# One correction operation in the first scan, early raw weights, and three unread products

## The chip, the cores and the metric

The kernel runs on one core of a Trainium2 chip. The metric is the device time of one execution in microseconds (us); lower is better. The engines are TensorE (PE in the profile, its weight loads PEld), VectorE (DVE), ScalarE (ACT), GpSimd (POOL) and SyncE (SP), whose queue issues the DMAs.

## The reference

Three stages follow one another, for 4 batches of 768 tokens. The first is a gated linear attention with 8 heads of 48 channels: per token a complex decay is normalised, a state is multiplied by it and takes up k v, and q reads it out.

```python
mag = np.sqrt(a_re * a_re + a_im * a_im)
scale = np.minimum(mag, 0.999) / (mag + 1e-06)
new_re = ar * S_re - ai * S_im          # per token t
new_im = ar * S_im + ai * S_re
S_re, S_im = new_re + kv, new_im
y[:, :, t] = np.einsum('bhd,bhde->bhe', q[:, :, t], S_re)
```

The second adds the real part of a two-dimensional Fourier transform to its input, normalises over the 384 channels and applies a two-layer network (384 to 1536 to 384). The third mixes over tokens (768 to 256 to 768) and then over channels again. All of it is float32.

## The kernel before, in words

The state is not stepped through token by token. For each chunk of 96 tokens the kernel forms the running complex product P of the decays, outward from the chunk's middle, in 48 steps plus one; q and k are multiplied by P or by its inverse, and the attention inside a chunk and from one chunk to the next is then matrix products. Four batches pass through the same program, and batch 0 has a scan of its own, `first_scan` (L330), which this change touches.

**The first scan.** 128 partitions hold head and chunk pairs, one half of them for each direction. `SL4` cuts the 49 steps into 12 slices of four and one of one, counted from 0. `st_a` loads the decays (`raw`) and q with k (`xx`), `st_b` to `st_e2` make the normalised multipliers A two slices ahead (ScalarE, GpSimd and VectorE together; L432 is GpSimd's last product of it, L401 the one before), and `st_f` is one step: two VectorE products (L453 into PSUM, L456 into `yt`) and their sum (L459) into P in PSUM. After a slice `st_s` squares P on ScalarE (L468) and makes |P|^2 (x) and 1/|P|^2 (r) with a logarithm and an exponential; GpSimd multiplies x by r (L473), which would be 1 if r were exact. `st_r` (L489) makes the correction (x r - 2) r, `st_x` (L495) multiplies the second half of `xx` by its negative, and `st_y` (L482) forms y, which is stored to DRAM (`kn`) and transposed on TensorE by `st_t` (L506). The function `vq` chains all VectorE operations of the scan in the order of the code, and `line_up` says which of them stand behind which step of the slice: eight places, two for each step, the first of the two ahead of the step's sum and the second behind it. L489 stands in place 6, ahead of the last sum, and L495 in place 7, behind it. In slices 8 to 11, `warm` (L316) puts two products with an identity into a PSUM tile that nobody reads.

**Around it.** After the scan `stage1` goes through 8 chunks of the attention (`ch_load`, `ch_sc`, `ch_u`, `ch_y`); the reloads of y from DRAM are L808, those of v L802. `stage2` makes the Fourier transform (`folds`, `mirrors`, `dft`, then products at L1115) and the normalisation, and `mlp`, `tok1` and `tok2` are the dense products (L999, L1021), from about 167 us to the end.

**Weights.** They come as 56 pieces of 64-bit numbers of 384 KB (`wL`, piece p, j). `convert` (L185) is a generator that a caller moves on by one stage at a time: the load (L190) into a tile of the tag T; two ScalarE operations on the halves (L198 to PSUM, L203 in place); a VectorE shift (L205); a GpSimd sum and a VectorE merge (L207, L210); then ScalarE makes a rounded first half (L216), GpSimd the rest (L217), and both are stored to `wscr` (L218), from where later batches load them. `early` is the list of the first eight pieces (p 0 to 3); their products go to tiles of the tags w1 and w2 (four buffers each, handed out in turn by `ws.place`). `tick` starts and moves conversions: two pieces at the start of the chunk loop and two after each of the first chunks (`CF`).

**The order of the work** is not that of the code. The framework plans a timeline ahead of the run: on each engine it takes, of the instructions that are ready by its plan, the one with the lowest number (`Prio`: conversions in the stream BACK come behind the first chain), and the engine then runs them strictly in that order. `after` adds an edge that holds for this planning only. Waits between engines and on buffers are put in by the framework.

Of the kernel before, what the change touches and what calls it, by code (L numbers as in the profile page):

```python
# [10 lines left out]
I32 = mybir.dt.int32  # L11
# [37 lines left out]
def with_ap(ap, offset, dims):  # L49
    return bass.AP(ap.tensor, ap.offset + offset, [list(ap.ap[0])] + [list(d) for d in dims])  # L50
# [3 lines left out]
def attn_fft_mixer_kernel(ctx: ExitStack, tc: tile.TileContext, aL, xL, vL, wL, qN, kN, vN, arN, aiN,  # L54
# [61 lines left out]
    def r32(ap):  # L116
        return ap.bitcast(F32)
# [48 lines left out]
    def marked(x):  # L166
        if stream[0] != CHAIN:
            mark[0] = x

    def after(x, y):  # L170
        tc.add_manual_dep(x.ins, y.ins.name, HOLD, reason="order of the streams")

    def hold(x):

        if mark[0] is not None:
            after(x, mark[0])
# [3 lines left out]
    def rest(x):  # L180

        if rests[0] is not None:
            after(x, rests[0])

    def convert(p, j, w=None, held=True, far=False):  # L185


        n = 384
        t = alloc("T", [128, 3 * n], I32, name="cvt")
        x = sp.dma_start(out=t[:, 0:2 * n], in_=wL32[p][:, 768 * j:768 * j + 768])  # L190
        if held:
            hold(x)
        yield
        raw = t[:, 0:2 * n].rearrange("p (n t) -> p n t", t=2)
        lo, hi, a = raw[:, :, 0], raw[:, :, 1], t[:, 2 * n:3 * n]
        if far:
            x = palloc("p" if far == 1 else "c", [128, n])
            se.activation(out=x, in_=hi.bitcast(F32), func=ACTF.Copy, scale=2.0 ** -112)  # L198
            top = hi = x.bitcast(I32)
        else:  # L200
            top = a
            se.activation(out=a.bitcast(F32), in_=hi.bitcast(F32), func=ACTF.Abs, scale=2.0 ** -112)
        se.activation(out=lo, in_=lo.bitcast(U32), func=ACTF.Copy, scale=2.0 ** -29)  # L203
        yield
        rest(ve.tensor_scalar(out=a, in0=top, scalar1=3, scalar2=None, op0=ALU.logical_shift_left))  # L205
        yield
        x = ge.tensor_tensor(out=a, in0=a, in1=lo, op=ALU.add)  # L207
        if rests[1] is not None:
            after(x, rests[1])
        rest(ve.scalar_tensor_tensor(out=a, in0=hi, scalar=-0x80000000, in1=a, op0=ALU.bitwise_and, op1=ALU.bitwise_or))  # L210
        if w is None:
            parts = t[:, 0:2 * n].bitcast(F32R).rearrange("p (k n) -> p k n", k=2)
        else:
            yield
            parts = w(p, j)
        se.copy(out=parts[:, 0, :], in_=a.bitcast(F32))  # L216
        ge.tensor_tensor(out=parts[:, 1, :], in0=a.bitcast(F32), in1=r32(parts[:, 0, :]), op=ALU.subtract)  # L217
        sp.dma_start(out=wscr[p][j], in_=r32(parts))  # L218

# [108 lines left out]
    def first_scan(t, knd, qk):  # L330
# [12 lines left out]
        def vq(x):  # L343

            if last[0] is not None:
                after(x, last[0])
            last[0] = x
            return x
# [114 lines left out]
        def st_s(i):  # L463

            d = t[i]
            n = d["n"]
            e = alloc("e", [128, n, 2, 48], name="ss")
            se.activation(out=e, in_=d["P"], func=ACTF.Square)  # L468
            x, r = e[:, :, 0, :], e[:, :, 1, :]
            ge.tensor_tensor(out=x, in0=x, in1=r, op=ALU.add)  # L470
            se.activation(out=r, in_=x, func=ACTF.Ln, bias=wee)
            se.activation(out=r, in_=r, func=ACTF.Exp, scale=-1.0)
            ge.tensor_tensor(out=x, in0=x, in1=r, op=ALU.mult)  # L473
            d["ss"] = e

        def st_y(i, k):
# [8 lines left out]

        def st_r(i):
            e = t[i]["ss"]
            o = with_ap(away[0], 192, [(48, t[i]["n"]), (1, 48)])
            vq(ve.scalar_tensor_tensor(out=o, in0=e[:, :, 0, :], scalar=-2.0, in1=e[:, :, 1, :], op0=ALU.add, op1=ALU.mult))  # L489
            t[i]["inv"] = o  # L490

        def st_x(i):
            d = t[i]
            x = d["xx"][:, :, 1, :]
            vq(ve.scalar_tensor_tensor(out=x, in0=d["inv"], scalar=-1.0, in1=x, op0=ALU.mult, op1=ALU.mult))  # L495

        def st_t(i, k):
            if not qk:
                qk.append(alloc("qk", [128, 12288], name="qkt"))
            qkt = qk[0][0:112]  # L500
            d = t[i]
            s0 = d["s0"]
            y = ybuf[k][i % 2]
            ps = palloc("s", [112, N4, 128])
            for j in range(N4):
                te.transpose(ps[:, j, :], y[:, j, 0:112], ident)  # L506

            def rows(ap, o, step, g=()):
                return with_ap(ap, o, [*g, (96, 8), (768, 8), (step, N4)])

            def cols(o, g=()):
                return with_ap(ps, o, [*g, (8, 8), (1, 8), (128, N4)])
            if k == 0:
                se.copy(out=rows(qkt, s0, 1, [(64 * 96 + 48, 2)]), in_=cols(0, [(64, 2)]))
            else:
                se.copy(out=rows(qkt, 64 * 96 + 47 - s0, -1), in_=cols(0))
                se.copy(out=rows(qkt, 48 + s0, 1), in_=cols(64))
# [30 lines left out]
        def line_up(i):  # L548

            fs = [[] for _ in range(8)]  # L550
            if 1 < i:
                fs[0] += [lambda: st_y(i - 2, 1), lambda: st_t(i - 2, 1)]
            if 0 < i < NS:
                fs[2] += [lambda: st_y(i - 1, 0), lambda: st_t(i - 1, 0)]
                fs[6] += [lambda: st_r(i - 1)]
                fs[7] += [lambda: st_x(i - 1)]
            if i + 2 < NS:
                at = (1, 4, 5)
                if not i:
                    at = (5, 6, 7)  # L560
                    fs[2] += [lambda: st_d(1)]
                    fs[3] += [lambda: part1(3), lambda: st_e1(1)]
                    fs[4] += [lambda: st_e2(1)]
                fs[at[0]] += [lambda: st_d(i + 2)]
                fs[at[1]] += [lambda: st_e1(i + 2)]
                fs[at[2]] += [lambda: st_e2(i + 2)]
            return [lambda f=f: [g() for g in f] for f in fs]
# [8 lines left out]
        part1(2)  # L576
        for i in range(NS):
            n = t[i]["n"]
            if i:
                part1(i + 3)  # L580
            fs = line_up(i)
            for j in range(n):
                st_f(i, j, fs[2 * j:2 * j + 2])
            st_s(i)
            for f in fs[2 * n:]:
                f()
            if WS <= i < 12:
                warm(W0, ybuf[0][i % 2].rearrange("p s c -> p (s c)"))
            if i == NS - 1:
                line_up(NS)[0]()  # L590
# [442 lines left out]
    def stage2(b, space):  # L1033
# [64 lines left out]
        folds(len(XP[b]) - 1, *XP[b][-1])  # L1098
        x = mirrors(*NR[1])
        if b == 0:  # L1100
            marked(x)
            rests[0], rests[1] = x, None
            for _ in range(5):
                tick(0)
            rests[0] = None
# [323 lines left out]
```

## Time and profile before

| | us |
|---|---|
| median of 3 runs (lowest, highest) | 1052.88 (1051.49, 1053.27) |
| profiled execution | 1054.68 |
| its span, first to last instruction | 1052.6 |
| TensorE products busy | 966.8 (92%) |
| VectorE busy | 744.2 (71%) |
| ScalarE busy | 511.5 (49%) |
| GpSimd busy | 392.2 (37%) |

The span is that of one profiled execution; what lies outside it (2.1 us) is start and end. Busy times of engines overlap. In the rows further down a timeline line gives start, duration, engine, line of the kernel, operation, output and inputs (buffer numbers left out), and in brackets the idle time before it with what ended it. The granted clock of TensorE is a share of 2.4 GHz: 1.00 is that level and 0.50 is 1.2 GHz.

### The profile page before, as it was taken

The page shows a single profiled execution, that of the slowest core. Times are in us where ns is not written, and L with a number is a line of the kernel's source. Part 1 is how long each engine was busy: PE and PEld are TensorE (multiplying, and loading weights), DVE is VectorE, ACT ScalarE, POOL GpSimd, SP SyncE. Part 2 cuts the span into 40 slices and gives each one's busy share as a digit, 9 for nine tenths or more (in the row PEclk, how much of TensorE's full clock was granted, in tenths as well). Part 3 has the DMA queues.
Part 4 walks back from the last instruction along what each step waited for, and adds up shares of the span by engine and source line. Part 5 has one row for each costly group of instructions (what it writes and reads, how often), then busy time and mean ns, then how long its engine had stood idle before and what let it go on. Part 6 is the DMA issues. An engine that isn't in the chain of part 4 may idle for free.

```text
span 1052.6 us, 21046 instructions
## 1 busy us (share of the span) xinstructions
PE 966.8 (92%) x7306; PEld 916.2 (87%) x7306; DVE 744.2 (71%) x2070; ACT 511.5 (49%) x1447; POOL 392.2 (37%) x541
## 2 busy tenths in 40 slices
PE   1469989998989899999999999999999999999997
PEld 0238877997889789999998999999899999999997
DVE  6986867998897697999768979984854433433332
ACT  6752557777875336788424757832252212111211
POOL 6632774565464772455237412414521002000000
PEclk9986899999989889999999999999999999999999
DMA  7226964777667743675654446665305344534422
GB/s 228 50 81 178 304 240 167 232 252 247 195 193 224 213 128 109 198 213 178 185 152 161 129 142 192 200 171 130 112 31 181 120 138 143 164 126 132 168 91 78
DMA packets 98337, 173.09 MB, mean 164 GB/s; under 512 B 10928, under 2 KB 57904, under 8 KB 97712
## 3 DMA queue, kind: packets, MB, share of 16 engines
q1 hardware_dynamic: 98224, 171.67, 52.7%
q8 instruction: 60, 0.98, 0.4%
q14 instruction: 53, 0.43, 0.1%
HBM read 132.31 MB, written 39.32 MB: 163 GB/s over the span
## 4 chain that ended last, share of the span: by engine, by line
PE 65%; DVE 15%; DMA 7%; ACT 5%; POOL 4%; issue 3%; SPq 1%; POOLq 0%; ACTq 0%; DVEq 0%
PE l L1021 23%; PE l L999 22%; DMA cvt<-wL 4%; PE s L817 2%; PE s L693 2%; PE s L1115 1%; PE l L1247 1%; DVE qkt L1064 1%; DVE h L1012 1%; DMA kn<-y 1%; PE s L1229 1%; DVE y L482 1%; DMA wscr<-w 1%; DVE cvt L210 1%; PE s L1247 1%
## 5 line engine op out<-in xcount | busy, mean ns | idle before, releaser
L1021 PE MATMUL l<-w,h 128*128 128x384 f32 x1728 | 327.9, 341 | 1.4 <-DVE h L1012 1.4
L999 PE MATMUL l<-th,w 128*128 128x384 f32 x1152 | 315.4, 342 | 2.3 <-DVE h L1012 2.0
L1021 PEld LDWEIGHTS l<-w,h 128*128 128x128 f32 x1728 | 301.0, 190 | 2.5 <-DVE h L1012 1.7
L999 PEld LDWEIGHTS l<-th,w 128*128 128x128 f32 x1152 | 210.2, 189 | 5.2 <-DVE h L1012 3.0
L999 PE MATMUL l<-tl,w 128*128 128x384 f32 x576 | 194.8, 338 | 0.0
L1003 ACT ACTIVATE h<-l 128x384 fp32r<-128x384 f32 x192 | 93.3, 487 | 207.5 <-PE l L999 206.8
L1024 DVE TENSOR_TENSOR u<-u,l 128x384 f32<-128x384 f32 x192 | 105.2, 548 | 71.7 <-PE l L1021 71.3
L1012 DVE SCALAR_TENSOR_TENSOR h<-l,h 128x384 fp32r<-128x384 f32 x160 | 88.3, 552 | 89.2 <-ACT h L1003 88.9
L999 PEld LDWEIGHTS l<-tl,w 128*128 128x128 f32 x576 | 109.0, 189 | 0.2
L207 POOL TENSOR_TENSOR cvt<-cvt 128x384 int32<-128x384 int32 x56 | 57.9, 1036 | 29.4 <-DVE cvt L205 25.7
L217 POOL TENSOR_TENSOR w<-cvt,w 128x384 fp32r<-128x384 f32 x44 | 45.8, 1042 | 49.4 <-ACT w L216 42.9
L1214 POOL TENSOR_TENSOR xl<-u,xh 128x384 fp32r<-128x384 f32 x18 | 18.1, 1014 | 96.3 <-ACT xh L1213 96.3
L203 ACT ACTIVATE cvt<-cvt 128x384 int32<-128x384 uint32 x56 | 31.2, 558 | 38.4 <-DMA cvt<-wL 38.4
L506 PE MATMUL s<-misc,y 128*112 128x128 f32 x64 | 14.5, 369 | 38.1 <-DVE y L482 32.8
L506 PEld LDWEIGHTS s<-misc,y 128*112 128x112 f32 x64 | 9.3, 176 | 44.6 <-POOL ss L470 21.0
L642 POOL TENSOR_TENSOR A<-raw,tm 128x144 f32<-128x144 f32 (+1 forms) x51 | 26.4, 517 | 53.3 <-DVE yt L667 19.1
L1010 POOL TENSOR_TENSOR h<-full,h 128x384 fp32r<-128x384 f32 x32 | 32.7, 1021 | 35.8 <-ACT full L1009 34.9
L666 DVE TENSOR_TENSOR p<-p,A 128x144 f32<-128x144 f32 x144 | 44.4, 308 | 1.3
L624 POOL TENSOR_TENSOR tm<-tm 128x144 f32<-128x144 f32 (+1 forms) x51 | 25.1, 494 | 51.3 <-ACT tm L623 48.8
L693 PE MATMUL s<-misc,y 128*112 128x128 f32 x222 | 36.5, 276 | 5.1 <-DVE y L677 3.6
L668 DVE TENSOR_TENSOR p<-p,yt 128x96 f32<-128x96 f32 x144 | 37.4, 260 | 2.3
L817 PE MATMUL s<-qkt 112*96 112x96 f32 x328 | 38.6, 266 | 0.2 <-DVE gt L785 0.2
(314 smaller groups left out, 1993.8 us busy)
## 6 DMA issues: line engine op xcount, KB each, us to landing
w<-wscr SPq DMA_DIRECT2D x180, 384.0 KB, 3.6
cvt<-wL SPq DMA_DIRECT2D x56, 384.0 KB, 4.6
wscr<-w SPq DMA_DIRECT2D x44, 384.0 KB, 3.3
Kn<-kn SPq DMA_DIRECT2D x56, 192.0 KB, 4.2
kn<-y SPq DMA_DIRECT2D x96, 96.0 KB, 2.4
raw<-aL SPq DMA_DIRECT2D x48, 144.0 KB, 3.6
xx<-xL SPq DMA_DIRECT2D x48, 144.0 KB, 3.8
V<-vL SPq DMA_DIRECT2D x32, 144.0 KB, 3.1
```

The lines of the kernel that those rows point to most:

```text
L207: x = ge.tensor_tensor(out=a, in0=a, in1=lo, op=ALU.add)
L217: ge.tensor_tensor(out=parts[:, 1, :], in0=a.bitcast(F32), in1=r32(parts[:, 0, :]), op=ALU.subtract)
L666: ve.tensor_tensor(out=cur, in0=prev, in1=A[:, j, 0:3, :], op=ALU.mult)
L668: ve.tensor_tensor(out=cur[:, 0:2, :], in0=cur[:, 0:2, :], in1=y, op=ALU.add)
L693: te.transpose(ps[:, j, :], y[:, j, 0:112], ident)
L817: te.matmul(out=ps[:, j, :], lhsT=K[:, hc, :], rhs=Q[:, hc, :])
L999: te.matmul(out=ps, lhsT=w1[:, wi, kt * 128:kt * 128 + 128], rhs=x[g][:, kt, :], start=(n == 0), stop=(n == 8))
L1003: x = se.activation(out=hi, in_=ps, func=ACTF.Relu)
L1010: ge.tensor_tensor(out=lo, in0=full, in1=r32(hi), op=ALU.subtract)
L1012: ve.scalar_tensor_tensor(out=lo, in0=ps, scalar=0.0, in1=r32(hi), op0=ALU.max, op1=ALU.subtract)
L1021: te.matmul(out=ps, lhsT=hs[m][:, hi, tt * 128:tt * 128 + 128], rhs=w2[:, wi, :], start=(n == 0), stop=(n == 8))
L1024: ve.tensor_tensor(out=u[tt], in0=u[tt], in1=ps, op=ALU.add)
```

## The change

Four edits. `st_s` gets a GpSimd product: r times the second half of `xx`, in place. `st_r` and `st_x` become one VectorE operation, (2 - x r) times that, in place 7. `preload` allocates eight tiles of w1 and w2, and in slices 5 to 8 issues two loads each of the early pieces into them; `convert` then reads the raw data there, keeps a T tile only for its intermediate, and its store to `wscr` is put on the list `kept`, which is stored after the last mirror of batch 0's `stage2`. And `st_t` puts three unread products of 512 columns behind the transposes of slice 11's first half.

```diff
+    ahead, kept = {}, []
+
+    def preload(n):
+
+        done = []
+        for p, j in early:
+            if (p, j) not in ahead and len(done) < n:
+                ahead[p, j] = alloc("w1" if j == 0 else "w2", [128, 768], I32, name="wr")
+                done.append(sp.dma_start(out=ahead[p, j], in_=wL32[p][:, 768 * j:768 * j + 768]))
+        return done
+
     def convert(p, j, w=None, held=True, far=False):
         n = 384
         t = alloc("T", [128, 3 * n], I32, name="cvt")
-        x = sp.dma_start(out=t[:, 0:2 * n], in_=wL32[p][:, 768 * j:768 * j + 768])
-        if held:
-            hold(x)
+        a = t[:, 2 * n:3 * n]
+        if (p, j) in ahead:
+            t = ahead[p, j]
+        else:
+            x = sp.dma_start(out=t[:, 0:2 * n], in_=wL32[p][:, 768 * j:768 * j + 768])
+            if held:
+                hold(x)
         yield
         raw = t[:, 0:2 * n].rearrange("p (n t) -> p n t", t=2)
-        lo, hi, a = raw[:, :, 0], raw[:, :, 1], t[:, 2 * n:3 * n]
+        lo, hi = raw[:, :, 0], raw[:, :, 1]
...
-        sp.dma_start(out=wscr[p][j], in_=r32(parts))
+        if (p, j) in ahead:
+            kept.append((wscr[p][j], r32(parts)))
+        else:
+            sp.dma_start(out=wscr[p][j], in_=r32(parts))
...
             ge.tensor_tensor(out=x, in0=x, in1=r, op=ALU.mult)
+            if d["m"]:
+                w = d["xx"][:, :, 1, :]
+                ge.tensor_tensor(out=w, in0=w, in1=r, op=ALU.mult)
             d["ss"] = e
...
         def st_r(i):
             e = t[i]["ss"]
-            o = with_ap(away[0], 192, [(48, t[i]["n"]), (1, 48)])
-            vq(ve.scalar_tensor_tensor(out=o, in0=e[:, :, 0, :], scalar=-2.0, in1=e[:, :, 1, :], op0=ALU.add, op1=ALU.mult))
-            t[i]["inv"] = o
-
-        def st_x(i):
-            d = t[i]
-            x = d["xx"][:, :, 1, :]
-            vq(ve.scalar_tensor_tensor(out=x, in0=d["inv"], scalar=-1.0, in1=x, op0=ALU.mult, op1=ALU.mult))
+            x = t[i]["xx"][:, :, 1, :]
+            vq(ve.scalar_tensor_tensor(out=x, in0=e[:, :, 0, :], scalar=2.0, in1=x, op0=ALU.subtract, op1=ALU.mult, reverse0=True))
...
             for j in range(N4):
-                te.transpose(ps[:, j, :], y[:, j, 0:112], ident)
+                tp = te.transpose(ps[:, j, :], y[:, j, 0:112], ident)
+            if 11 <= i and (i, k) != (11, 1):
+                warm(3 if i == 11 else 1, y.rearrange("p s c -> p (s c)"), tp)
...
-                fs[6] += [lambda: st_r(i - 1)]
-                fs[7] += [lambda: st_x(i - 1)]
+                fs[7] += [lambda: st_r(i - 1)]
...
         for i in range(NS):
             n = t[i]["n"]
+            if i in (5, 6, 7, 8):
+                for x in preload(2):
+                    after(x, t[i - 1]["scan"])
...
         x = mirrors(*NR[1])
         if b == 0:
+            for o, v in kept:
+                after(sp.dma_start(out=o, in_=v), x)
             marked(x)
```

## Rows read from the trace of the kernel before

**Rows 1.** Windows by stage: length, busy us (count) per engine, clock, DMA share, GB/s.

```profile
21.39:52.89 31.50, 14.74 (x51) 9.47 (x52) 29.29 (x114) 24.23 (x73) 20.42 (x30) 1.00 0.22 51
52.89:75.00 22.11, 13.88 (x51) 6.38 (x50) 20.33 (x79) 11.54 (x37) 8.01 (x15) 0.92 0.28 70
75.00:95.00 20.00, 17.18 (x148) 14.73 (x149) 9.76 (x30) 5.45 (x18) 2.95 (x5) 0.50 0.45 135
95.00:140.00 45.00, 41.18 (x573) 36.55 (x572) 37.47 (x86) 23.59 (x54) 27.14 (x27) 0.92 0.96 305
140.00:167.40 27.40, 22.68 (x127) 17.64 (x126) 20.18 (x60) 16.57 (x48) 19.60 (x24) 0.94 0.46 172
167.40:1052.60 885.20, 856.01 (x6362) 830.72 (x6360) 613.60 (x1656) 415.61 (x1182) 300.98 (x412) 0.99 0.52 162
```

**Rows 2.** Timeline of VectorE, a steady slice's ends; last two from slice 11.

```profile
35.70 0.25 DVE L456 TENSOR_TENSOR yt<-p,A 128x96 f32<-128x96 f32 x1
...
36.32 0.27 DVE L459 TENSOR_TENSOR p<-l,yt 128x96 f32<-128x96 f32 x1
36.49 0.35 DVE L495 SCALAR_TENSOR_TENSOR xx<-l,xx 128x192 f32<-128x192 f32 x1
37.14 0.27 DVE L453 TENSOR_TENSOR l<-p,A 128x96 f32<-128x96 f32 x1 [0.30 <-ACT ss L468]
...
42.39 0.27 DVE L453 TENSOR_TENSOR l<-l,A 128x96 f32<-128x96 f32 x1 [0.30 <-ACT ss L468]
...
71.08 0.25 DVE L456 TENSOR_TENSOR yt<-l,A 128x96 f32<-128x96 f32 x1
71.36 0.27 DVE L459 TENSOR_TENSOR l<-l,yt 128x96 f32<-128x96 f32 x1
```

**Rows 3.** Instructions of line L489: duration ns min/median/max, first and last start.

```profile
L489 DVE SCALAR_TENSOR_TENSOR l<-ss x12: 366/392/848, 19.7 to 75.9; 128x192 f32<-128x192 f32 x12
```

**Rows 4.** Timeline of VectorE, the last step of slice 8.

```profile
56.62 0.25 DVE L456 TENSOR_TENSOR yt<-l,A 128x96 f32<-128x96 f32 x1
...
57.70 0.27 DVE L459 TENSOR_TENSOR l<-l,yt 128x96 f32<-128x96 f32 x1
```

**Rows 5.** Timeline of GpSimd, two steady slices and slice 8.

```profile
36.02 0.94 POOL L432 TENSOR_TENSOR A<-A,both 128x384 f32<-128x384 f32 x1
...
38.80 0.59 POOL L473 TENSOR_TENSOR ss<-ss 128x192 f32<-128x192 f32 x1 [0.48 <-ACT ss L472]
40.53 0.78 POOL L401 TENSOR_TENSOR tm<-tm 128x192 f32<-128x192 f32 x1 [1.14 <-ACT tm L399]
...
56.61 0.82 POOL L432 TENSOR_TENSOR A<-A,both 128x384 f32<-128x384 f32 x1 [1.08 <-DVE A L428]
```

**Rows 6.** Timeline of VectorE, the last y of the scan.

```profile
76.74 0.56 DVE L482 TENSOR_TENSOR y<-xx,l 128x384 f32<-128x384 f32 x1
```

**Rows 7.** Chain of work that ended last, from 64 to 115 us: start, us, what.

```profile
78.22 2.94 DMA kn<-y
...
81.26 2.82 DMA Kn<-kn
```

**Rows 8.** Waits from 68 to 170 us: us in total, times, longest us.

```profile
ACT cvt L203 <- DMA cvt<-wL: 17.0, 10, 4.3
```

**Rows 9.** Timeline of VectorE, the first product (L853) of four chunks.

```profile
94.09 0.56 DVE L853 TENSOR_TENSOR yc<-l,gm 48x384 f32<-48x384 f32 x1 [2.04 <-PE l L848]
...
99.38 0.56 DVE L853 TENSOR_TENSOR yc<-l,gm 48x384 f32<-48x384 f32 x1
...
107.24 0.56 DVE L853 TENSOR_TENSOR yc<-l,gm 48x384 f32<-48x384 f32 x1
...
113.38 0.56 DVE L853 TENSOR_TENSOR yc<-l,gm 48x384 f32<-48x384 f32 x1
```

**Rows 10.** Timeline of TensorE, unread products of slices 8 and 9, two each.

```profile
50.84 3.60 PE L321 MATMUL l<-y,misc 128*128 128x512 f32 x4
...
55.61 1.88 PE L321 MATMUL l<-y,misc 128*128 128x512 f32 x4
```

## The prediction

> **What bounds the kernel now.** I read the busy table by stage first, then each stage's own timeline. From 167.4 us on, the dense products fill TensorE (856 of 885 us at clock 0.99), and the change takes nothing out of them [rows 1]. So the question is how early that stretch can begin. Ahead of it lie the first scan (to 75 us), the chunk loop and transforms (75 to 140), and the second transform (140 to 167.4). In the scan TensorE is idle half of the time while VectorE works 29.3 of 31.5 us: the scan is VectorE's. From 75 to 95 TensorE is nearly always busy, but at 0.50, the 1.2 GHz level. From 95 to 140 the DMA engines are 0.96 busy [rows 1].
>
> In the scan's timeline one slice of four tokens takes 42.39 - 37.14 = 5.25 us. Its last step has the correction L489 between yt (L456, 35.70) and the sum L459 (36.32): 0.62 us, where the bare pair takes 71.36 - 71.08 = 0.28. After the sum the next slice starts 0.82 us later, held by ScalarE's square of the same product bank; L495 (0.35 us) lies inside that wait and costs nothing [rows 2].
>
> **The change part by part.** *One correction operation.* L489 and L495 become one operation in L495's place, behind the sum; GpSimd gets one more product per slice. What goes from VectorE's path is 0.62 - 0.28 = 0.34 us a slice. What may come back: L495 reads one operand from PSUM, the new operation reads two from SBUF, as L489 did. L489 takes 0.39 us in the median but up to 0.85 [rows 3]. In the slice from 52.89 the stretch from yt to the sum is 57.70 - 56.62 = 1.08 us instead of 0.62 [rows 4], and GpSimd's L432 runs from 56.61 to 57.43 just then; the sum starts 0.27 us after L432's end [rows 5]. The new operation's place in a steady slice is 0.17 us behind the sum, and L432 runs there (36.02 to 36.96).
>
> So I count the twelve uses by their neighbours. Steady slices (2 to 7, six): the sum moves from 36.32 to 35.98, ScalarE would release the next slice at 35.98 + 0.82 = 36.80, but L432, which without L489 in its way takes 0.82 and ends at 36.84, holds the new operation. If the next slice follows L432's end by 0.27, as in rows 4, it starts at 37.11 and 0.03 us is gained; if the new operation were free, 0.34. The next step doesn't read its result, and independent steps here start before their forerunner ends (L495 0.10 us before the sum's end [rows 2]), so I take 0.15: 6 x 0.15 = 0.9 us, bounds 0.2 and 2.0. Slices 8 and 9: 1.08 - 0.28 = 0.80 goes; L432 then holds the new operation to 57.70, but the square holds the next slice to 56.62 + 0.28 + 0.82 = 57.72 anyway: 2 x 0.80 = 1.6. Slice 1 has the same collision, but GpSimd's queue is fuller there: 0.5 of 0.8. Slices 10 and 11 have no long L432: 2 x 0.3 = 0.6. In slice 12 nothing covers: a GpSimd product more (0.59 us, as L473 [rows 5]), one operation of 0.39 less: +0.2. Scan: -0.9 - 1.6 - 0.5 - 0.6 + 0.2 = -3.4 us, bounds -4.8 and -2.0.
>
> The trace shows L489 at 0.85 where it meets L432 and 0.39 elsewhere [rows 3 to 5]. The Trainium skill's "SBUF — State Buffer" (Who interferes with whom) says that a VectorE instruction with two SBUF inputs and a GpSimd instruction that reads SBUF exclude each other for the whole instruction; the trace agrees in these three slices. By the rule the merged operation pays in every steady slice for what L495 didn't; without it the six would give 2.0 and the sum would be 1.1 larger.
>
> GpSimd's twelve products cost nothing in the steady slices: it idles 1.14 us ahead of L401 [rows 5], and the new 0.59 us fits behind L473 (38.80 to 39.39). Without that cover it is 0.59 a slice, 7 us in all.
>
> *Eight raw weights early.* Eight loads of 384 KB go out in slices 5 to 8, where the DMA engines are 0.22 to 0.28 busy [rows 1]. Eight issues delay SP's stores of the scan by well under 1 us each; these have a whole slice of slack, since their buffers alternate. What they leave: first, the two loads that stood in SP's queue at the scan's end. The last y is done at 76.74 + 0.56 = 77.30 us [rows 6], its store goes out only at 78.22, and store and reload (2.94 and 2.82 us) lead straight to the chunk loop [rows 7]. I give 0.5 of the 0.9 us back, bounds 0 and 0.9. Second, the loop itself: ScalarE waits for these loads 17.0 us in ten places, 4.3 at most [rows 8], VectorE's conversion step stands behind it in order, and the loop's steps behind that. Undisturbed, a chunk takes VectorE 99.38 - 94.09 = 5.29 us; the two after it take 107.24 - 99.38 = 7.86 and 113.38 - 107.24 = 6.14 [rows 9]. With the data there both should come to 5.29: 2.57 + 0.85 = 3.4 us, bounds 0 (TensorE or the chunk's own loads hold it instead) and 4.1.
>
> The raw data lies in the buffers that the products later take, in the same order, so the conversions wait for nothing new. The eight stores of the halves move behind the last mirror (about 140 us): 3 MB, some 10 us at the 305 GB/s of rows 1, into a stretch where the DMA engines are 0.46 busy. That room covers them; without it the two loads of that time come up to 10 us later, and ScalarE's transform copies queue behind their conversions.
>
> *Three products in the last slice.* Each is half of a pair of L321: 1.88 / 2 = 0.94 us at 2.4 GHz, 1.8 at 1.2 [rows 10], so 2.8 or 5.4 us on TensorE, ahead of the last transposes, which are due about 1.5 us after the ones they follow. That is 1.3 or 3.9 us late. TensorE has about 1 us of room before the chunk loop's first product, and at the higher level its score products ahead of it are twice as fast. I take 0, bounds -2.5 (below) and +2.
>
> Sum: -3.4 - 0.5 - 3.4 = -7.3 us. The profiled execution took 1054.68 us, 2.1 of it outside its span of 1052.6; so 1047.4 in its terms, and against the median of 1052.88 about 1045.5 us.
>
> **The rivals.** (1) *The clock holds through the first chunk.* For it: the added products come where TensorE is nearly idle and the clock falls (0.92 before 75 us, 0.50 after). Against: they are followed by a wait for the reload. At 2.4 GHz the 17.2 us of work in 75 to 95 [rows 1] would halve, but VectorE's 5.29 us a chunk and the reload stay: 2.5 us more. 1043. (2) *The chunk loop doesn't shrink.* Something else, the reloads or TensorE at 1.2 GHz, holds it: only scan and start, -3.9, 1049. (3) *Given back before the dense products.* The stretch from 140 us converts other weights in the same queues, with the moved stores beside it; if they set its end, 1 us remains: 1052. (4) *Slower: ScalarE waits for raw data inside the scan.* The instructions are ordered by a planned timeline; with the data planned to be there, the first conversion step (L203) may be put between the scan's ScalarE steps, and if a load lands later than planned, the square and so VectorE stand behind it. At the 17.0 / 10 = 1.7 us of rows 8 for each of eight it is 13.6 - 7.3 = +6.3: 1059. It decides above 7.3 / 8 = 0.9 us a load. Against it: those waits were in a crowded stretch, here the engines are a quarter busy.
>
> **How the numbers follow.** Forecast 0.43, (1) 0.17, (2) 0.18, (3) 0.10, (4) 0.08, else 0.04. A measurement of this kernel tells 0.2% (2.1 us) from no change. Faster by more: forecast, (1), (2) and a little of (3), 0.80. Within: most of (3), 0.10. Slower: 0.10. Range: the forecast's own is 1043 to 1048; with (1) below and (2) and half of (3) above it is 1040 to 1052.
>
> **What would show it.** A steady slice of 5.1 us, the sum 0.28 us after yt in every slice, the new operation longer than 0.35 where it meets L432; scan slices 8 and 9 near 4.8 us; no wait of L203 on a load before 115 us; chunk periods of 5.3 us; the first dense product near 160 us. Wrong it would be if steady slices reach 5.25, if ScalarE waits for a load before 75 us, or if the dense products start early and the span doesn't follow.

## The result and the profile after

The kernel after takes 1040.74 us (median of 4 runs, 1037.56 to 1042.85), the one before 1053.08 beside it (1051.49 to 1053.56): a ratio of 0.9883, 95% interval [0.9855, 0.9911]. Forecast were 1045.5 us, with a range of 1040 to 1052. The profiled run took 1040.36 us, its span is 1038.6.

Windows of the profile after by stage, against [rows 1] (length, then busy us and count of PE, PEld, DVE, ACT and POOL, clock, DMA share, GB/s):

```profile
20.27:51.39 31.12, 14.52 (x51) 9.25 (x52) 28.91 (x110) 26.71 (x81) 23.17 (x37) 1.00 0.55 152
51.39:75.00 23.61, 17.01 (x59) 9.61 (x58) 19.74 (x77) 14.15 (x43) 11.93 (x23) 0.86 0.25 57
75.00:95.00 20.00, 18.49 (x304) 15.72 (x303) 15.64 (x42) 5.22 (x14) 5.64 (x7) 1.00 0.54 129
95.00:130.00 35.00, 31.21 (x428) 27.82 (x426) 33.62 (x74) 18.37 (x44) 24.03 (x26) 1.00 0.80 258
130.00:156.20 26.20, 21.05 (x115) 16.00 (x113) 19.11 (x57) 16.02 (x45) 18.50 (x23) 0.93 0.66 253
156.20:1038.60 882.40, 852.33 (x6362) 825.05 (x6360) 613.42 (x1655) 415.25 (x1182) 300.51 (x412) 0.99 0.53 162
```

The third row is what the sum did not have: from 75 to 95 us the granted clock is 1.00, the 2.4 GHz level, where it was 0.50, and TensorE gets through 304 products instead of 148. The early loads show in the first row's 152 GB/s. The dense stretch is the same work: 6362 products in 882 us instead of 885.

Executions of one kernel differ, and the clock differs with them: the four of the kernel after took 1037.56 to 1042.85 us at mean granted clocks of 0.993 to 0.985. Windows, landmarks and chunk periods below come from one profiled execution of each kernel. In these the start of slice 1 alone lies anywhere from 14.71 to 15.76 us, and it does not follow the edits (15.33 in the kernel before, 15.00 in `w_only` and 15.38 in `mp`, both further down), so parts of half a microsecond aren't told apart at a landmark.

The same landmarks in both traces, in us from the span's start; "expected" is the sum of the prediction up to that point:

| | before | after | moved | expected |
|---|---|---|---|---|
| last y of the scan | 76.74 | 74.69 | -2.05 | -3.4 |
| issue of its store | 78.22 | 75.27 | -2.95 | -3.9 |
| first state product of chunk 0 (L832, now L851) | 84.21 | 81.39 | -2.82 | -3.9 |
| VectorE's first product of chunk 0 (L853, now L872) | 87.88 | 82.55 | -5.33 | -3.9 |
| the same of chunk 2 | 99.38 | 90.96 | -8.42 | -3.9 |
| the same of chunk 4 | 113.38 | 101.21 | -12.17 | -7.3 |
| first dense product | 167.39 | 156.16 | -11.23 | -7.3 |
| end of the span | 1052.6 | 1038.6 | -14.0 | -7.3 |

VectorE's first product of chunks 0 to 4 in the profile after, against [rows 9] (start, us, engine, line, operation; brackets hold the idle time before):

```profile
82.55 0.56 DVE L872 TENSOR_TENSOR yc<-l,gm 48x384 f32<-48x384 f32 x1 [2.05 <-PE l L852]
...
86.75 0.56 DVE L872 TENSOR_TENSOR yc<-l,gm 48x384 f32<-48x384 f32 x1
...
90.96 0.56 DVE L872 TENSOR_TENSOR yc<-l,gm 48x384 f32<-48x384 f32 x1
...
96.08 0.56 DVE L872 TENSOR_TENSOR yc<-l,gm 48x384 f32<-48x384 f32 x1
...
101.21 0.56 DVE L872 TENSOR_TENSOR yc<-l,gm 48x384 f32<-48x384 f32 x1
```

The two periods that the loads were to shorten are 5.12 and 5.13 us, as forecast. The two ahead of them are 4.20 and 4.21 instead of 6.21 and 5.29: in these only one of VectorE's two conversion lines stands (L220 or L225), so 5.29 us was not its floor there.

The wait on the raw data, against [rows 8], from 65 to 170 us (us in total, times, longest):

```profile
ACT cvt L218 <- DMA cvt<-wL: 3.1, 3, 1.5
```

TensorE ahead of chunk 0 in the kernel before:

```profile
80.32 1.57 PE L817 MATMUL s<-qkt 112*96 112x96 f32 x8
81.69 1.49 PE L817 MATMUL c<-qkt 112*96 112x96 f32 x8
...
84.21 0.31 PE L832 MATMUL l<-V,Kn 96*64 96x48 f32 x1 [1.03 <-DMA Kn<-kn]
...
85.20 1.60 PE L817 MATMUL s<-qkt 112*96 112x96 f32 x8
```

And in the kernel after, with the unread products (L339) ahead of it:

```profile
72.95 3.30 PE L339 MATMUL l<-y,misc 128*128 128x512 f32 x6
76.09 0.60 PE L521 MATMUL s<-misc,y 128*112 128x128 f32 x4
...
78.18 0.84 PE L836 MATMUL c<-qkt 112*96 112x96 f32 x8
78.99 0.92 PE L836 MATMUL s<-qkt 112*96 112x96 f32 x8
81.39 0.23 PE L851 MATMUL l<-V,Kn 96*64 96x48 f32 x1 [1.49 <-issue]
```

The order is another. Before, the second half of chunk 0's score products stands among its state products, behind the seventh of sixteen (the group at 85.20), behind the wait for the reload. After, it stands ahead of them (78.99), where TensorE would only wait. The first VectorE product of chunk 0 follows the first state product by 3.67 us before and by 1.16 us after. No line of the diff asks for this: the planner chose it. That is the 2.5 us between the third and the fourth row of the table.

### The profile page after: what moved, and what is told of

Same layout as the page of the kernel before. It is cut to its first block, busy times and chain, and to the rows that moved or that the text cites. A ratio compares the mean times of both kernels' runs of the same rounds, so it can differ in the third digit from the quotient of the medians.

```text
span 1038.6 us, 21023 instructions
## 1 busy us (share of the span) xinstructions
PE 955.7 (92%) x7312; PEld 904.1 (87%) x7312; DVE 744.0 (72%) x2058; ACT 510.4 (49%) x1447; POOL 397.1 (38%) x553
## 4 chain that ended last, share of the span: by engine, by line
PE 62%; DVE 15%; DMA 7%; ACT 6%; POOL 5%; issue 4%; SPq 1%; POOLq 0%; ACTq 0%; DVEq 0%
PE l L1040 22%; PE l L1018 22%; DMA cvt<-wL 3%; PE s L836 1%; PE s L712 1%; PE s L1136 1%; PE l L1268 1%; DVE cvt L225 1%; DMA V<-vL 1%; DVE h L1031 1%; DMA raw<-aL 1%; DVE cvt L220 1%; DVE qkt L1083 1%; PE s L1250 1%; POOL w L232 1%
## 5 line engine op out<-in xcount | busy, mean ns | idle before, releaser
L222 POOL TENSOR_TENSOR cvt<-cvt 128x384 int32<-128x384 int32 x48 | 50.3, 1050 | 14.3 <-DVE cvt L220 11.8
L218 ACT ACTIVATE cvt<-cvt 128x384 int32<-128x384 uint32 x48 | 26.5, 557 | 27.4 <-DMA cvt<-wL 27.2
L872 POOL TENSOR_TENSOR yc<-Aa,gm 48x384 f32<-48x384 f32 x18 | 19.4, 1078 | 49.2 <-DVE Aa L862 48.9
```

## The experiments

Three kernels do one part of the change each, a fourth all but the unread products. Diffs are against the kernel after where nothing else is said.

**m_only**: the merged correction alone.

```diff
-            if 11 <= i and (i, k) != (11, 1):
-                warm(3 if i == 11 else 1, ...)
-            if i in (5, 6, 7, 8):
+            if i in ():
```

> The merged correction operation alone, no early loads, no three products. Stage theory (each edit keeps the share that the changed kernel's trace shows in its stage): the scan ends 2 to 3 us earlier, the clock in 75 to 95 us stays at 0.50, the chunk loop keeps its two long periods (7.9 and 6.1 us): -2.5 us against the kernel before. Rival (the port takes it all back): steady slices at 5.25 us and less than -1.

Measured: 1049.60 us, ratio 0.997 [0.9947, 0.9993]. Last y at 73.11, 3.6 us earlier (expected in the sum: 3.4), of which 0.6 is there already when slice 1 starts and can't be put down to the edit; slices 4 to 7 of 5.00 us, clock 0.50 from 75 to 90, first dense product at 165.7. The scan was sized about rightly; more than half of it is gone by the dense products, which start 1.7 us earlier.

**p_only**: early loads and late stores alone; the old pair of operations stands in its old places, and the GpSimd product is gone.

```diff
-            x = t[i]["xx"][:, :, 1, :]
-            vq(ve.scalar_tensor_tensor(... op0=ALU.subtract, op1=ALU.mult, reverse0=True))
+            o = with_ap(away[0], 192, ...)
+            vq(ve.scalar_tensor_tensor(out=o, ... op0=ALU.add, op1=ALU.mult))
...
-                warm(3 if i == 11 else 1, ...)
```

> The early raw weights and their late stores alone, with the old two correction operations and no three products. Stage theory: the last y's store goes out 0.9 us earlier, the two long chunk periods (7.9 and 6.1) become 5.3, the scan is 0.3 us longer by the conversion steps between ScalarE's scan steps, the clock stays at 0.50 until the loop is under way: -4 us. Rival (the loop is held by TensorE at 1.2 GHz and by its own reloads): -1.5 or less.

Measured: 1047.02 us, 0.9961 [0.9938, 0.9983]. Periods of chunks 2 and 3: 4.89 and 5.34 us instead of 7.86 and 6.14. But the last y comes at 78.80, 2.1 us later than before (0.4 of it by the start of slice 1): ScalarE's first conversion steps are planned between the scan's own, and slices 4 to 7 take 5.51 us instead of 5.25. The first dense product comes at 161.0. TensorE has the new order here, without any unread product.

**w_only**: the three products alone, merge and loads undone as in the two kernels above; the diff is against the kernel before.

```diff
+            if 11 <= i and (i, k) != (11, 1):
+                warm(3 if i == 11 else 1, y.rearrange(...), tp)
```

> The three unread products alone. Clock theory: they run at 1.2 GHz (about 5 us), the clock stands at 1.00 from about 80 us on, and the first two chunks take 8.4 instead of 11.5 us: -3 us, unless what follows waits for its loads anyway. Rival (the loads hold the loop): the clock rises as well but the waits on loads grow by as much, and the span moves by less than 1 us.

Measured: 1044.18 us, 0.9935 [0.9909, 0.996]. Clock 1.00 from 75 to 100 us, first chunk periods of 4.20 and 4.20, first dense product at 161.1. The term that I had set to nothing has the lowest ratio of the three taken alone, though its interval overlaps that of `p_only`. TensorE has the new order here too.

**mp**: the change without the three products.

```diff
-                warm(3 if i == 11 else 1, y.rearrange(...), tp)
```

> The changed kernel without the three products. Clock theory: the first two chunks are back at about 11.5 us and the clock at 0.50 up to about 90 us: 4 to 5 us slower than the changed kernel, -7.5 against the kernel before. Rival (the clock falls and rises by the spacing of the work and the faster scan alone keeps it): within 1.5 us of the changed kernel, -11.

Measured: 1044.46 us, 0.9927 [0.9897, 0.9957]; last y at 75.25, but the first product of chunk 0 at 85.86, at a clock of 0.50 up to 90 us, and the first dense product at 165.1. This one has the old order, so the 8.9 us between its first dense product and that of the kernel after are order and clock together.

**w1**: the kernel after with one product for three.

```diff
-                warm(3 if i == 11 else 1, ...)
+                warm(1 if i == 11 else 1, ...)
```

> The changed kernel with one unread product in slice 11 instead of three. Clock theory (the three keep TensorE busy long enough that the clock stands at 1.00 when the chunk loop begins): one product, 1 to 2 us, does not do it; the clock is 0.50 in 80 to 85 us, the first two chunk periods are 6 instead of 4.2 us, and the kernel is 3 to 5 us slower than the changed one, -8 us against before. Rival (any product there will do): clock 1.00, periods 4.2, the changed kernel's time.

Measured: 1043.17 us, 0.9927 [0.9901, 0.9952]. Windows from 75 to 95 us, columns as above:

```profile
75.00:80.00 5.00, 4.30 (x47) 3.60 (x46) 3.30 (x18) 1.67 (x7) 0.29 (x1) 0.86 0.56 110
80.00:85.00 5.00, 3.37 (x56) 3.18 (x58) 2.55 (x5) 0.00 (x0) 0.00 (x0) 0.82 0.48 131
85.00:90.00 5.00, 5.00 (x49) 4.22 (x46) 2.13 (x6) 0.58 (x1) 1.97 (x2) 0.50 0.62 133
90.00:95.00 5.00, 5.00 (x89) 4.55 (x88) 4.87 (x10) 2.02 (x5) 0.41 (x1) 1.00 0.26 74
```

It has the new order, and VectorE starts chunk 0 at 82.78, as after (82.55). Then the clock falls to 0.50 and chunk 0 takes 7.04 us instead of 4.20; the first dense product is at 159.0 instead of 156.2. With the order as it is, the clock that the other two products hold is worth 2.8 us between these two executions. That is a price from one pair: the profiled execution of `w1` had the lowest clock of its nine (0.979, and 1046.15 us; the nine reach down to 1037.31 us at 0.991), and the intervals of the two ratios overlap.

**held**: ScalarE's first conversion steps planned behind the scan's last VectorE operation.

```diff
+            if (p, j) in ahead:
+                after(z, over[0])        # both ScalarE steps
...
+        over[0] = last[0]                # ahead of st_end()
```

> The changed kernel with the first two ScalarE steps of the eight early conversions planned behind the scan's last VectorE operation. Queue theory (these steps, put between the scan's ScalarE steps, cost the scan about 0.1 us in slices 5 to 7 and 1 us in its tail): no L218 or L213 step before the last y; slices 5 to 7 near 5.13 us instead of 5.24; the last y 1.2 us earlier; the span 1 us shorter, unless the conversions are then late for the chunk loop. Rival (they only fill gaps): the last y at the same time, within 0.3 us.

Measured: 1049.59 us, 0.9992 [0.9975, 1.0008]. The scan did what it should: slices 4 to 7 of 5.00 us, last y at 73.49, 1.2 us earlier than after. ScalarE just behind it:

```profile
74.89 3.15 ACT L221 ACTIVATE wr<-wr 128x384 int32<-128x384 uint32 x7
77.94 0.22 ACT L545 COPY ends<-l 128x96 f32<-128x96 f32 x1
```

Seven conversion steps stand ahead of the copy that the prefix products need (75.55 in the kernel after). These products slip behind the reload in TensorE's order, to 82.2, the clock is 0.50 from 80 to 85, VectorE starts chunk 0 at 86.19, 3.6 us later than after, and the first dense product comes at 164.1; the time is that of the kernel before.

**actx**: the correction off VectorE, its subtraction on ScalarE and a third product on GpSimd.

```diff
+                se.activation(out=x, in_=x, func=ACTF.Copy, scale=-1.0, bias=2.0)
                 ge.tensor_tensor(out=w, in0=w, in1=r, op=ALU.mult)
+                ge.tensor_tensor(out=w, in0=w, in1=x, op=ALU.mult)
...
-                fs[7] += [lambda: st_r(i - 1)]
```

> The changed kernel with the correction taken off VectorE: ScalarE forms 2 - x r, and a third GpSimd product applies it. Port theory (the merged operation reads two SBUF operands and excludes GpSimd's L450, so the steady slice loses what L489 gave back): without it no 0.94 us L450 and no 0.9 us wait in the scan's last step; steady slices 4.9 to 5.0 instead of 5.13 to 5.24 us, the last y 1 us earlier, if GpSimd's queue, 0.6 us longer per slice, has room. Rival (ScalarE's square and its queue set the slice): 5.2 as now.

Measured: 1040.10 us, 0.9901 [0.9874, 0.9928]. The scan is longer: VectorE waits for the square eleven times, 7.7 us in all, the last y comes at 79.10 and the first dense product at 161.1, 4.9 us later than after. Its time is that of the kernel after all the same; the table further down shows why that is no merit of this edit.

**direct**: the early products stored at once, not behind the mirror.

```diff
-        if (p, j) in ahead:
-            kept.append((wscr[p][j], r32(parts)))
-        else:
-            sp.dma_start(out=wscr[p][j], in_=r32(parts))
+        sp.dma_start(out=wscr[p][j], in_=r32(parts))
```

> The changed kernel with the early products stored to DRAM at once, as before, instead of behind the last mirror. Load theory (what the chunk loop gains is the loads that no longer stand before ScalarE, not the stores): the chunk periods stay at 5.1 to 5.2 us and the span within 1.5 us of the changed kernel. Rival (the stores' 3 MB crowd the loop's own reloads): one or two periods of 6 us and more, 2 to 3 us slower.

Measured: 1042.30 us, 0.9925 [0.9898, 0.9953], first dense product at 157.9 instead of 156.2. The chunk periods to be kept at 5.1 to 5.2 are 5.12 to 5.13: the load theory holds for them. The late stores are worth 1.7 us at the mark, in one pair of executions; in the time the intervals of the two ratios overlap, and no difference is shown.

The last four take order and products apart. **bo**: the kernel before, with nothing but the order on TensorE.

```diff
+                if b == 0 and c == 0:
+                    ch_sc(1, 0)
                 ch_u(c)
...
+                    for q in st["scs"]:       # each state product of chunk 0
+                        after(z, q)           # behind the score products
```

> The kernel before, with one change of order on TensorE: the second half of chunk 0's score products (four of 96x96) stands ahead of chunk 0's sixteen state products, where the planner had put it among them, behind the seventh. No merged correction, no early loads, no unread products. The planner gave the kernels with the unread products this order too, so it may be part of what these seemed to earn. Theory A (order): in the kernel before the first VectorE product of chunk 0 starts 87.88 - 84.21 = 3.67 us after the first state product, in those with the new order 1.16 us after it. Some 2.5 us less, where the score products' own 1.5 us at the lower clock are then done while TensorE waits for the reload: first chunk product near 85.5, 1050.5 us. Theory B (the clock alone): the clock stays at 0.50 from 75 to 90, the first state product moves back by as much as the score products take, and the first chunk product stays near 87.5: 1053 us.

Measured: 1047.22 us, 0.9945 [0.9923, 0.9967]. TensorE ahead of chunk 0 in it:

```profile
79.68 1.57 PE L817 MATMUL s<-qkt 112*96 112x96 f32 x8
81.05 1.49 PE L817 MATMUL c<-qkt 112*96 112x96 f32 x8
82.33 1.49 PE L817 MATMUL s<-qkt 112*96 112x96 f32 x8
```

Its windows from 80 to 90 us:

```profile
80.00:85.00 5.00, 5.00 (x50) 4.83 (x50) 2.93 (x13) 0.26 (x1) 0.00 (x0) 0.50 0.33 97
85.00:90.00 5.00, 5.00 (x84) 4.49 (x82) 4.21 (x9) 0.58 (x1) 1.02 (x2) 0.96 0.64 161
```

VectorE starts chunk 0 at 85.66 (theory A: 85.5) and the first dense product comes 4.0 us earlier. Theory B falls. Of the 2.2 us at chunk 0's start 0.4 were there at the last y (76.38 instead of 76.74). A had still priced the end of it too low, at 2.5 us, for the clock follows: TensorE, busy for the whole of 80 to 85 where it was busy for 3.96 us before, is at 0.96 from 85 to 90, where the kernel before stays at 0.50 up to 95, and chunk 0 takes VectorE 3.74 us instead of 6.21. This is the one difference of order that the times show by themselves: all ten executions took 1044.11 to 1049.87, and the interval lies below 1.

**mpo**: `mp` with the same edit as `bo`.

```diff
+                if b == 0 and c == 0:
+                    ch_sc(1, 0)
                 ch_u(c)
```

> The merged correction and the early loads, without the three unread products, but with TensorE's order of the kernel after (chunk 0's score products all ahead of its state products). It holds the order fixed and takes the products away. Against the same kernel with the old order (first chunk product 85.86, 1044.5 us): A (order) says first chunk product 2.5 us earlier, near 83.4, and 1042 us; B (clock alone) says nothing changes, 85.9 and 1044.5 us. What then still parts it from the kernel after (82.55 and 1040.7 us) is the clock: the first two chunk periods of 6.2 and 5.6 us at 0.50 against 4.2 and 4.2 us, 3.4 us.

Measured: VectorE starts chunk 0 at 83.19 (A: 83.4) instead of 85.86, the first dense product at 158.8 instead of 165.1. The clock is 0.81 from 80 to 85 and 1.00 behind that, and the first two chunk periods are 4.57 and 4.89: the 6.2 and 5.6 us expected at 0.50 did not come. And the time is 1051.99 us, 1.0003 [0.9983, 1.0022]: A's 1042 failed by 10 us. Nothing ahead of the dense products explains that.

**mid**: the kernel after with the old order.

```diff
                     after(z, q)
+                    if h == 3:
+                        ch_sc(0, 1, z)     # among the state products again
```

> The kernel after with the old order on TensorE: the second half of chunk 0's score products stands among its state products again, behind the seventh. It keeps the three unread products and so, if they are what holds it, the clock of 1.00 from 75 us on. A (order): at the higher clock the inserted products cost half of what they cost before, 1.2 us: first chunk product near 83.7, 1042 us. B (clock alone): 82.6 and 1040.7 us. If the clock falls to 0.50 again from 77 us on, the order is what kept it, and the products earn nothing by themselves: 1044.5 us.

Measured: 1046.68 us, 0.9934 [0.9905, 0.9964]. Its windows from 75 to 90 us:

```profile
75.00:80.00 5.00, 4.35 (x42) 3.05 (x40) 2.99 (x17) 1.67 (x7) 0.29 (x1) 1.00 0.58 110
80.00:85.00 5.00, 3.61 (x43) 3.21 (x41) 1.18 (x3) 0.00 (x0) 0.00 (x0) 0.64 0.25 73
85.00:90.00 5.00, 5.00 (x62) 4.65 (x59) 3.62 (x7) 0.58 (x1) 1.41 (x2) 0.50 0.41 94
```

The third case of the expectation came. In this execution the three products hold the clock to 80 us and then it falls, VectorE starts chunk 0 at 85.27, chunk 0 takes 8.46 us, and the first dense product comes at 167.2, where that of `mp` comes at 165.1: with the old order the products earned nothing in it. (The planner also put half of chunk 0's output products among chunk 1's state products here, so the 2.1 us are not all the products'.) It is weak evidence for the kernel as such: the profiled execution, of 1048.52 us, had with one other the lowest mean clock of the twelve (0.974), and the twelve reach from 1038.27 us at 0.986 to 1050.95 us. Whether the clock fell at this place in the others too isn't on record.

**heldgo**: `held`, but until the operation on the flag behind the prefix products, with the new order forced.

```diff
-        if b == 0:
-            tick(CF[0])
         st_g2()
+        if b == 0:
+            tick(CF[0])
...
+            over[0] = ve.tensor_scalar(out=gate[:, b:b + 1], ...)
```

> An attempt at a better one: the kernel after, in which the first ScalarE steps of the early conversions wait for the gate of the first scan (the operation on the flag behind the scan's prefix products) instead of standing between the scan's own ScalarE steps, and with TensorE's order of the kernel after forced. When they were held only until the scan's last VectorE operation, the scan was 1.2 us shorter, but seven of them stood in ScalarE's queue ahead of the copies that the prefix products need, and all was given back. If that was the cause: steady slices of 5.00 us, last y near 73.5, first chunk product near 81.4, and the conversions in the chunk loop, where ScalarE has room: 1039.5 us. If the conversions are now late (their VectorE steps stand in the loop's own queue), chunk periods 1 to 5 grow beyond 5.1 us and it takes 1042 us or more.

Measured: 1041.87 us, 0.9899 [0.9865, 0.9933]: no better than after. The last y comes at 73.50, as expected; VectorE starts chunk 0 at 84.04 and not at 81.4. ScalarE ahead of it:

```profile
77.95 0.26 ACT L805 COPY gt<-s 48x128 f32<-48x128 f32 x1
...
79.58 3.23 ACT L221 ACTIVATE wr<-wr 128x384 int32<-128x384 uint32 x7
82.84 0.26 ACT L805 COPY gt<-s 48x128 f32<-48x128 f32 x1
```

The flag's operation falls between the two copies, so the seven steps stand ahead of the second one: the mishap of `held` once more, one copy later. Holding them until that copy was not tried.

**Why `mpo` and `actx` miss.** Each edit makes the planner lay the whole program anew. I compared the order of each trace's instructions in the dense stretch with that of the kernel before, by operation, tiles and the line's text. In five others (marked "as before") all 1656 operations of VectorE come in the same order, and of TensorE's 6362 records at most 28 are out of place, where single records missing from a trace shift the rest. In the rest at least 239 of VectorE's and 579 of TensorE's are out of place.

| | later order | first dense product | median | median less first dense product |
|---|---|---|---|---|
| before | | 167.4 | 1052.9 | 885.5 |
| bo | as before | 163.4 | 1047.2 | 883.8 |
| p_only | as before | 161.0 | 1047.0 | 886.0 |
| w1 | as before | 159.0 | 1043.2 | 884.2 |
| direct | as before | 157.9 | 1042.3 | 884.4 |
| after | as before | 156.2 | 1040.7 | 884.5 |
| mpo | other | 158.8 | 1052.0 | 893.2 |
| held | other | 164.1 | 1049.6 | 885.5 |
| heldgo | other | 157.4 | 1041.9 | 884.5 |
| m_only | other | 165.7 | 1049.6 | 883.9 |
| w_only | other | 161.1 | 1044.2 | 883.1 |
| mid | other | 167.2 | 1046.7 | 879.5 |
| mp | other | 165.1 | 1044.5 | 879.4 |
| actx | other | 161.1 | 1040.1 | 879.0 |

Where the later order is the same, what lies behind the first dense product takes 883.8 to 886.0 us, over 11 us of starts: a gain there is passed on whole. (The median of the kernel before, taken anew beside each group of runs, was 1051.1 to 1053.1.) Where it differs it takes 879 to 893. That the order is the cause of that spread isn't shown by itself (no kernel changed it alone). For it speak `mp` and `actx`: they share one of the other orders, all 1656 operations of VectorE, and take 879.4 and 879.0 us behind starts that are 4 us apart. So against the kernel after the time of `actx` gets some 5 us back in that stretch, and the edits are compared at the first dense product. The column mixes a landmark of one execution with a median of several, so differences of 2 us in it can't be read.

## Why the prediction was right, and where it was not

The sign and the range held. The number did not hold as well: 12.3 us were gained where 7.3 were forecast, the time lies below the 1043 to 1048 that was the forecast's own, and 0.7 us inside the range. Of the parts the sum had priced, the loop came as forecast and the scan fell short; what carried the time past them is a term the sum put at 0 and an order that it did not have. That the time is within the range at all owes something to rival (1), which held its lower end open.

At the first dense product the parts can be put in a row, from `bo` on each with the new order: before 167.4, `bo` 163.4, `p_only` 161.0, `mpo` 158.8, after 156.2. Along this row the order is worth 4.0 us, the loads 2.4, the merged correction 2.2, the products 2.6. Along another row they are other sizes: with the old order the merged correction is worth 1.7 (`m_only`), the loads on top of it 0.6 (`mp`), and the order then 6.3 (`mpo`). The parts lean on each other, and the sum of the row is more certain than its terms.

*The scan*, -3.4: measured -3.6 alone (`m_only`; -3.0 from the start of slice 1), -2.05 in the whole change (-1.5). VectorE, the ends of three steps of the profile after, against [rows 2]; the last sum of a slice stands 0.28 us behind yt, as forecast:

```profile
29.47 0.25 DVE L474 TENSOR_TENSOR yt<-p,A 128x96 f32<-128x96 f32 x1
29.75 0.27 DVE L477 TENSOR_TENSOR p<-l,yt 128x96 f32<-128x96 f32 x1
29.92 0.91 DVE L510 SCALAR_TENSOR_TENSOR xx<-ss,xx 128x192 f32<-128x192 f32 x1
30.75 0.25 DVE L471 TENSOR_TENSOR l<-p,A 128x96 f32<-128x96 f32 x1
...
34.75 0.27 DVE L477 TENSOR_TENSOR p<-l,yt 128x96 f32<-128x96 f32 x1
34.92 0.36 DVE L510 SCALAR_TENSOR_TENSOR xx<-ss,xx 128x192 f32<-128x192 f32 x1
35.67 0.27 DVE L471 TENSOR_TENSOR l<-p,A 128x96 f32<-128x96 f32 x1 [0.39 <-ACT ss L486]
```

GpSimd in these two slices, against [rows 5]:

```profile
29.79 0.82 POOL L450 TENSOR_TENSOR A<-A,both 128x384 f32<-128x384 f32 x1
...
35.03 0.94 POOL L450 TENSOR_TENSOR A<-A,both 128x384 f32<-128x384 f32 x1
```

Of the merged operation and L450, the one that comes second is the longer one: 0.91 us against 0.36, or 0.94 against 0.82. The Trainium skill's "SBUF — State Buffer" (Who interferes with whom) has the two exclude each other, and these rows agree. But in `m_only` and `held` the operation takes 0.91 at the end of slices 3 to 7, and slices 4 to 7 still are 5.00 us, 0.25 shorter: the wait for the square covers most of it. Slice 2 takes 5.05 and slice 3 5.43, so the six gain 1.0 us in `m_only`, as forecast (0.9). In the whole change they gain 0.38 (20.27 to 51.39): slices 5 to 7 take 5.23 to 5.25 us, the length that I had named as a sign of being wrong. Slices 8 and 9 gained 1.05 of the 1.6. VectorE at the end of slice 8, against [rows 4]:

```profile
55.43 0.24 DVE L474 TENSOR_TENSOR yt<-l,A 128x96 f32<-128x96 f32 x1
55.71 0.27 DVE L477 TENSOR_TENSOR l<-l,yt 128x96 f32<-128x96 f32 x1
55.88 0.58 DVE L510 SCALAR_TENSOR_TENSOR xx<-ss,xx 128x192 f32<-128x192 f32 x1
```

The sum follows yt by 0.28, and the next slice starts at 56.53, 1.10 behind yt, as worked out (0.28 + 0.82). The missing 0.3 went earlier in the slice: it takes 5.14 us here and 4.81 in `held`, without the conversion steps. Slice 1 gained 0.60 (0.5), slices 10 and 11 0.50 (0.6); the 0.52 ahead of slice 1 are not in the sum and can't be put down to the edit. Slice 12 lost 1.0 and not 0.2; alone (`m_only`) the merge loses 0.5 there. ScalarE there:

```profile
71.36 0.52 ACT L213 ACTIVATE p<-wr 128x384 f32<-128x384 f32 x1
...
72.54 0.38 ACT L490 ACTIVATE ss<-ss 128x192 f32<-128x192 f32 x1
```

And VectorE behind it:

```profile
74.24 0.36 DVE L510 SCALAR_TENSOR_TENSOR xx<-ss,xx 128x192 f32<-128x192 f32 x1 [2.52 <-POOL xx L494]
74.69 0.56 DVE L503 TENSOR_TENSOR y<-xx,l 128x384 f32<-128x384 f32 x1
```

A conversion step (L213) stands ahead of the scan's exponential (L490), whose result the chain to the last y waits for. This is rival (4) at small size: no wait on a load in the scan, but steps between the scan's own, here and in slices 5 to 8, that cost 1.5 us in all: from the start of slice 1 to the last y it is 59.9 us in the kernel after and 58.4 in both `m_only` and `held`. I had asked whether the data would be late and not what the steps themselves take; the sum had no term for them. (Conversions first wait for a load at 103.8 us, 1.5 us long, and not behind 115 as I had it: that sign failed, and the wait falls behind the chunks that the loads were to shorten.)

*The start*, -0.5: all of the 0.9 came. SP's queue in the profile after, against [rows 6, 7]:

```profile
74.51 0.46 SPq L827 DMA_DIRECT2D Kn<-kn  x1
75.27 0.45 SPq L505 DMA_DIRECT2D kn<-y  x1
```

*The chunk loop*, -3.4: the periods of chunks 2 and 3 fell by 3.75 us, as forecast. It is not all the loads': without any early load they add up to 11.8 us in `bo` and 11.9 in `w_only`, against 14.0 before and 10.25 after. The late stores go out from 124.75 us on in the kernel after, not at 140.

*Three products*, 0: this step failed. They took 3.30 us in the kernel after and 2.74 in `w_only`. (That one takes 1.8 at 1.2 GHz was read from a row, 50.84 to 54.44, for which the profile shows a granted clock of 1.00; no row of before shows that price.) I had taken rival (1), the clock that holds, as one case with 0.17 and 2.5 us; it came, and three pairs of executions price it: 2.8 us against `w1` (one product left), 2.6 against `mpo` (none) and 2.3 for `w_only` against `bo`. Of the 2.6 only 1.2 are there when VectorE starts chunk 5 (106.33 against 107.56); the rest arises behind it. The sum had no term for the order ahead of chunk 0 either: `mp`, the change without the products, has the old one, and the kernel after has the new. The products are not the only way to it, for `p_only` has it without them. My objection, "they are followed by a wait for the reload", was a fair one: the 1.49 us in front of L851 are there, the clock held over them in the kernel after and over 1.38 us in `w_only`, and it fell with a wait of 1.39 in `mid` and of 1.80 in `w1`. From 80 to 85 TensorE is busy 3.6 us in the kernel after and in `mid`, but from 77 to 82 it is 3.5 us in the one and 3.0 in the other, where it idles 0.65 us more just ahead of 79.30. Why the clock stays at 1.00 in the one and is 0.64 in the other from 80 to 85 isn't settled.

*Passing on*: what came at the first dense product came out in the time (-11.2 there, -12.3 in the median). That step was right, and it holds for the kernels whose later order is that of before.

## What to carry to other kernels

Where a planner orders the program, compare the order of the instructions before putting a gain down to an edit: here moving four products ahead of a wait was worth 4.0 us taken alone, and no line of the diff asked for it. Work that is free of dependencies belongs in front of an engine's wait and not behind it. Judge an edit at the first landmark behind it, since the whole time also carries what the planner did elsewhere; and look at the clock of every execution before reading much from the one that was profiled.

## What the runs showed of the hardware

The merged correction takes 0.36 us, and 0.91 where GpSimd's product started first; slices 4 to 7 are 5.00 us with the blocked one and were 5.25 with the old, unblocked pair. From 85 to 90 us TensorE's granted clock was 0.50 before, and 0.96 with four score products moved ahead of a wait and none added; TensorE had been busy for 5.00 us of the 5 ahead, instead of 3.96. With one unread product in place of three it was 0.82 from 80 to 85 and 0.50 from 85 to 90, with three it was 1.00 in both, each in one execution. Executions of one and the same kernel differ as well: `mid` took 1049.85 us at a mean clock of 0.974 and 1038.27 at 0.986.
